# Windowed attention into a GELU MLP: from the fourth tile of tokens on, the first MLP product as seven block products instead of eight, with queries and keys loaded by pairs of heads

## The chip, the cores and the metric

The kernel runs on one core of one Trainium2 chip. The time is the device time of one execution in microseconds (us), median of three runs. The core has the engines PE (TensorE matmuls; PEld is its weight loads), DVE (VectorE), ACT (ScalarE), POOL (GpSimd), and SP, whose queue issues the DMAs.

## The reference

```python
# q, k, v: (8, 8, 576, 64) f32; w_in: (512, 2048), w_out: (2048, 512) f32
scores = scale * np.matmul(q, k.transpose(0, 1, 3, 2))
rel = pos[:, None] - pos[None, :]
scores = np.where((rel >= 0) & (rel < 128), scores + slopes * -abs(rel), -1e9)
attn = softmax(scores);  o = np.matmul(attn, v)
x = o.transpose(0, 2, 1, 3).reshape(8 * 576, 512)        # 4608 tokens
h = x @ w_in
return (0.5 * h * (1.0 + erf(h / sqrt(2)))) @ w_out      # (4608, 512)
```

## The kernel before

The 4608 tokens are cut into nine tiles of 512 (`t` = 0 to 8; the fourth tile is `t` = 3). The attention of batch 0 and the second product of tile 0 run in float32; elsewhere every float32 factor is kept as a float16 high part and a float16 low part, and a product is three matmuls (high by high, low by high, high by low) that add up in PSUM.

A tile has two phases. The h phase, `mlp_in(t, fc)` for 16 blocks `fc` of 128 hidden columns, adds 12 matmuls of 512 moving columns (4 blocks of the contraction by 3 terms) in one PSUM bank with the tag "mm" (four banks). ACT then applies GELU out of PSUM into a float32 buffer `g32` (tag "ob", three buffers), POOL writes its scaled float16 high part into `g`, and DVE writes the low part (`low_part`). The o phase, `mlp_out(t, tb, fc)`, computes four blocks of 128 tokens, each of 16 by 3 matmuls of 512 columns with `g` as the stationary operand, and stores them through a buffer of the same tag "ob".

Between these matmuls the attention of batch `b = t + 1` is placed by step: `scores(unit(b, hp))` of a pair of heads `hp` (54 small matmuls; DVE takes them out of PSUM with scale and bias into `s`), `softmax` (DVE maxima `nmax`, ACT exponentials, POOL high parts and DVE low parts in `e_main`, and two DMA transposes into `et`), and `weigh` (matmuls of `et` and `vbuf` into the bank `av`, then ACT and DVE write the high and low parts of `x` of this tile and the next one). `load_qk(b + 1)` fetches all queries and all keys of a batch at once into two large buffers (tag "ld"); `split_qk` measures them on DVE, sets a scale by a power of two, and writes the high and low parts into `qbuf` and `kbuf`. `split_v` does the same with the values.

The steps of one tile and the step at which each unit starts are a table (`SCORES_AT`, `WEIGH_AT`), but the order of instructions on each engine is set by a list scheduler that runs at build time: it may move an instruction ahead of others by its estimate of when the operands are there. Each engine then runs its list strictly in order, and SP issues the DMAs in order too.

## Time and profile before

| what | us |
|---|---|
| median of three runs | 959.24 (958.87 to 961.88) |
| the profiled execution | 957.65 |
| its span on the core | 955.8 |
| PE busy | 920.2 (96%) |
| DVE busy | 634.8 (66%) |
| ACT busy | 449.5 (47%) |
| POOL busy | 253.5 (27%) |

The profile is one execution. A line of a group gives the source line, the engine, the operation, what it writes and reads, the shapes, the count, then the busy time and the mean duration (ns) of one, then the idle time of the engine just before such instructions and what ended it. In the table by stretch each engine has its busy time in us and the number of its instructions; PEclk is the granted share of the TensorE clock. The phases stand cleanly apart in the trace: the tiles start at 187.9 (`t` = 1), 294.1, 395.8, 493.7, 592.2, 689.2, 786.1 and 869.0 us, and the last matmul starts at 951.7 us. A matmul's end is modelled, so time per matmul is read from start to start.

### The profile page before, as it was taken

The numbers are of one execution on the slowest core, as the hardware profiler recorded it, in microseconds if no ns is written. First come the engines' busy times: TensorE is split into PE (matmuls) and PEld (weight loads), VectorE is DVE, ScalarE is ACT, GpSimd is POOL, SyncE is SP. The second block draws the span as 40 slices with busy tenths as digits, with TensorE's granted clock in tenths as the row PEclk, the third lists the DMA queues.
The fourth block names the chain that finished last, engine by engine and source line by source line (L and its number), as shares of the span: only waits on it lengthen the run. The fifth ranks groups of instructions, "written<-read, shape, count | busy, mean of one in ns | idle before, by whom it ended". The sixth has DMA issues, their size and how long they took to land.

```text
span 955.8 us, 17566 instructions
## 1 busy us (share of the span) xinstructions
PE 920.2 (96%) x7036; PEld 450.0 (47%) x7036; DVE 634.8 (66%) x1254; ACT 449.5 (47%) x957; POOL 253.5 (27%) x516
## 2 busy tenths in 40 slices
PE   6979999899798999999999999999999999999998
PEld 3554444444454445444544445444544454444443
DVE  6899989769886978588767876777566722201200
ACT  5977556344563665256626643664366313101200
POOL 1010004323441533144313530353044312201200
PEclk8999999899999999999999999999999999999999
DMA  9527615762367424713371346245312430000000
GB/s 324 199 96 244 222 50 74 132 188 100 72 135 166 76 51 106 193 32 66 79 193 45 66 95 171 56 79 95 73 28 51 86 81 1 1 23 23 0 12 34
DMA packets 172451, 91.18 MB, mean 95 GB/s; under 512 B 132561, under 2 KB 153169, under 8 KB 172241
## 3 DMA queue, kind: packets, MB, share of 16 engines
q1 hardware_dynamic: 172368, 90.06, 38.3%
q8 instruction: 55, 0.90, 0.4%
q14 instruction: 28, 0.22, 0.1%
HBM read 46.53 MB, written 9.44 MB: 59 GB/s over the span
## 4 chain that ended last, share of the span: by engine, by line
PE 68%; DVE 8%; ACT 4%; DMA 3%; issue 2%; POOL 1%; SPq 0%; POOLq 0%; ACTq 0%; DVEq 0%
PE o L622 31%; PE h L584 29%; PE av L540 4%; PE sc L399 3%; DMA et<-e_main 2%; ACT s L494 2%; DVE e_main L145 2%; DVE s L421 1%; DVE g L145 1%; DVE nmax L491 1%; DVE stq L213 1%; POOL e_main L500 1%; DMA q<-qp 1%; DVE wo L145 1%; DMA v<-vp 1%
## 5 line engine op out<-in xcount | busy, mean ns | idle before, releaser
L584 PE MATMUL h<-x,wi 128*128 128x512 f16 x1728 | 381.8, 379 | 5.0 <-ACT g L600 3.3
L584 PEld LDWEIGHTS <-wi 128*128 128x128 f16 x1728 | 166.2, 98 | 205.8 <-issue 7.3
L622 PE MATMUL o<-wo,g 128*128 128x512 f16 x1152 | 260.2, 380 | 0.0
L622 PEld LDWEIGHTS <-g 128*128 128x128 f16 x1536 | 145.9, 98 | 175.2 <-issue 0.7
L601 POOL TENSOR_SCALAR g<-g,sg 128x512 f16<-128x512 f32 x128 | 104.2, 818 | 286.1 <-ACT g L600 280.4
L494 ACT ACTIVATE s<-s,nmax 128x192 f32<-128x192 f32 x252 | 111.2, 442 | 121.4 <-DVE nmax L491 114.4
L145 DVE SCALAR_TENSOR_TENSOR g<-g,sg,g 128x512 f16<-128x512 f32 x128 | 106.1, 841 | 90.4 <-POOL g L601 90.3
L500 POOL TENSOR_SCALAR e_main<-s,z 128x192 f16<-128x192 f32 x252 | 121.4, 499 | 126.1 <-issue 43.6
L600 ACT ACTIVATE g<-h,gs 128x512 f32<-128x512 f32 x128 | 86.0, 686 | 135.0 <-PE h L584 108.6
L145 DVE SCALAR_TENSOR_TENSOR e_main<-s,z,e_main 128x192 f16<-128x192 f32 x252 | 111.0, 482 | 15.3 <-POOL e_main L500 14.8
L622 PE MATMUL o<-wo_first,g 128*128 128x512 f16 x384 | 88.3, 379 | 0.0
L399 PE MATMUL sc<-kbuf,qbuf 64*64 64x192 f16 (+1 forms) x1656 | 73.3, 261 | 8.5 <-DMA kbuf<-kp 4.6
L421 DVE SCALAR_TENSOR_TENSOR s<-sc,cs,bias_h 128x384 f32<-128x384 f32 x112 | 63.6, 607 | 12.2 <-PE sc L399 12.0
L553 ACT ACTIVATE x<-av,cx 128x448 f16<-128x448 f32 (+6 forms) x52 | 23.8, 475 | 91.7 <-PE av L540 91.5
L491 DVE TENSOR_REDUCE nmax<-s 128x5 f32<-128x960 f32 (+1 forms) x56 | 58.5, 1044 | 2.7 <-DVE s L421 0.5
L619 PE MATMUL o<-zo,g 128*128 128x512 f32 x128 | 58.1, 606 | 0.0
L540 PE MATMUL av<-et,vbuf 128*64 128x128 f16 (+1 forms) x1680 | 46.0, 215 | 11.9 <-DMA et<-e_main 11.1
L426 POOL MEMSET s<- 64x128 f32 (+1 forms) x112 | 19.1, 171 | 135.1 <-DVE s L421 134.5
L630 ACT ACTIVATE ob<-o,so 128x512 f32<-128x512 f32 x16 | 10.8, 677 | 90.8 <-PE o L622 90.7
L399 PEld LDWEIGHTS <-qbuf 64*64 64x64 f16 x1512 | 36.2, 107 | 36.8 <-issue 33.5
L540 PEld LDWEIGHTS <-vbuf 128*64 128x64 f16 x1680 | 43.0, 114 | 22.2 <-issue 18.4
L632 DVE TENSOR_SCALAR ob<-o,so 128x512 f32<-128x512 f32 x16 | 11.9, 744 | 60.0 <-PE o L622 60.0
(129 smaller groups left out, 737.5 us busy)
## 6 DMA issues: line engine op xcount, KB each, us to landing
v<-vp SPq DMA_DIRECT2D x32, 320.0 KB, 5.2
out<-ob SPq DMA_DIRECT2D x36, 256.0 KB, 2.0
raw<-w_in SPq DMA_DIRECT2D x8, 1024.0 KB, 14.2
raw<-w_out SPq DMA_DIRECT2D x8, 1024.0 KB, 5.0
q<-qp SPq DMA_DIRECT2D x7, 1152.0 KB, 6.1
k<-kp SPq DMA_DIRECT2D x7, 1152.0 KB, 6.0
qbuf<-qp SPq DMA_DIRECT2D x4, 288.0 KB, 4.7
kbuf<-kp SPq DMA_DIRECT2D x4, 288.0 KB, 5.0
```

The source lines that it names most:

```text
L145: nc.vector.scalar_tensor_tensor(out=dst, in0=src, scalar=scale, in1=high, op0=ALU.mult, op1=ALU.subtract)
L399: nc.tensor.matmul(ps[bank][o, n, 0:W], a, m, start=(i == 0), stop=(i == len(terms) - 1 and b > 0), skip_group_check=True,)
L421: nc.vector.scalar_tensor_tensor(out=s[:, bank[0] : bank[0] + k, :], in0=ps[bank][:, 0:k, 0:W], scalar=cs, in1=bias.broadcast_to([P, k, W] ...
L491: nc.vector.tensor_reduce(out=nmax[:, r], in_=s[:, r], axis=AX.X, op=ALU.max, negate=True)
L494: nc.scalar.activation(s[:, i, :], s[:, i, :], AF.Exp, bias=nmax[:, i : i + 1], accum_out=z[:, i : i + 1])
L500: nc.gpsimd.tensor_scalar(e[:, i, 0, c], s[:, i], z[:, i : i + 1], 1.0, op0=ALU.mult, op1=ALU.mult)
L540: nc.tensor.matmul(av[r, (j - blocks[0]) * QB : (j - blocks[0] + len(js)) * QB], v32s[b][:, hp, kb, r] if b < EXACT else vbuf[:, vi, hp, k ...
L584: nc.tensor.matmul(ph, wi[n][:, a, cc, k * P : (k + 1) * P], x[:, cc, b, :], start=(i == 0), stop=(i == 3 * NCC - 1),)
L600: nc.scalar.activation(g32, ph, AF.Gelu, scale=gsc[t, n])
L601: nc.gpsimd.tensor_scalar(g[:, r, 0], g32, gsg[t, n], 1.0, op0=ALU.mult, op1=ALU.mult)
L619: nc.tensor.matmul(o, g[:, r, c], zo[n][:, n % 2, k * DM : (k + 1) * DM], start=(fc == 0), stop=(fc == NFC - 1))
L622: nc.tensor.matmul(o, g[:, r, a, c], wo[n][:, b, k, :], start=(fc == 0 and i == 0), stop=(fc == NFC - 1 and i == 2),)
```

## The change

Both halves of a block of the first product's operands are used in a scheme of seven products for a 2 by 2 by 2 product of blocks. Two token halves (`HT` = 256), two halves of the contraction (the blocks `2i` and `2i + 1` for `i` = 0, 1), and two blocks of 256 hidden columns (`wi[2d]` and `wi[2d + 1]`) make eight block products; for `t` >= `FAST` = 3 a class `Seven(t, d)`, `d` = 0 to 3, computes them with seven, `p1` to `p7`, each of 12 matmuls with 256 moving columns. They need sums of blocks:

- of the weights, formed once while tile 2 is computed (`sums_of_weights(d, i)`, eight calls, at the steps `SUMS_AT`). One sum replaces half of `wi[2d + 1]`; three go to DRAM (`stored`) and come back, for each `d` of each tile, by `stream` into `ldbuf`.
- of `x`, formed for each tile by `sums_of_x(t + 1, i)` during the tile before (POOL five additions, ACT high part, DVE low part).

The products of one `d` share two PSUM banks, `u` and `v`. A result is copied out, and the next product is added to what stands in the bank: `u` holds p1, then p1+p6, then also p7, then also p4; `v` holds p2, then (overwritten) p5, then also p3. ACT copies `u` out three times per `d`, DVE adds `v` to a copy three times, and four GELUs of [128, 512] with POOL and DVE parts follow as before.

Queries and keys of the batches from `WHOLE` = 3 on are held two pairs at a time (in half of `qbuf` and `kbuf`), because `ldbuf` is needed for the sums. From batch 4 on each pair is loaded twice: once into `src32[1]` to be measured, once into `src32[0]` to be split. One DVE chain `scales(b)` finds the scales of values, queries and keys together. The two weight blocks of a pair share a scale. `maxima` is taken out of `softmax`, and in the fast tiles the softmax of units whose scores fall in the h phase is held back until the o phase (`waiting`). The table `AT` moves the first unit of the next batch into the end of the tile before: tile 2 has five units of scores, tile 6 has three.

```diff
+WHOLE = 3
+FAST = 3
+HT = TT // 2
...
+    def load_pair(b, hp, n):
+        nc.sync.dma_start(src32[n][:, 0], qp[b, hp])
+        nc.sync.dma_start(src32[n][:, 1], kp_[b, hp])
+    def measure(b, hp):
...
+        absmax(stats[b][:, :, hp], src32[1])
...
+    def split_pair(b, hp):
...
+            nc.scalar.activation(a[:, 0:S], src, AF.Copy, scale=sc[:, n : n + 1])
+            low_part(a[:, S : 2 * S], src, sc[:, n : n + 1], a[:, 0:S])
...
+    def sums_of_weights(d, i):
+        r = ldbuf[:, LD : LD + 1024].rearrange("p (m c f) -> p m c f", m=2, c=2)
...
+        for m in range(2):
+            w = wi[2 * d + m]
+            nc.gpsimd.tensor_tensor(
+                out=r[:, m], in0=w[:, 0, 2 * i : 2 * i + 2], in1=w[:, 1, 2 * i : 2 * i + 2], op=ALU.add
+            )
+        b11, b21, b12, b22 = r[:, 0, 0], r[:, 0, 1], r[:, 1, 0], r[:, 1, 1]
+        nc.gpsimd.tensor_tensor(out=b11, in0=b12, in1=b11, op=ALU.subtract)
...
+        nc.scalar.copy(hi, flat)
+        nc.vector.tensor_tensor(out=lo, in0=flat, in1=hi, op=ALU.subtract)
+        nc.sync.dma_start(wi[2 * d + 1][:, :, 2 * i], st[:, :, 0])
+        for n, k in ((T2, 3), (T3, 2), (T4, 1)):
+            nc.sync.dma_start(stored[n, d, :, :, i], st[:, :, k])
+    def stream(n, d):
+        nc.sync.dma_start(streams[n], stored[n, d])
+    def sums_of_x(t, i):
+        x = x_tile(t)[:, 2 * i : 2 * i + 2]
+        r = pool.tile([P, 2, TT], F32, tag="s", name=f"r{t}_{i}", bufs=2)
+        nc.gpsimd.tensor_tensor(out=r, in0=x[:, :, 0], in1=x[:, :, 1], op=ALU.add)
...
+        nc.scalar.copy(hi, flat)
+        nc.vector.tensor_tensor(out=lo, in0=flat, in1=hi, op=ALU.subtract)
+    class Seven:
...
+        def add(self, ps, w, m, first):
+            n = 0
+            for k in range(2):
+                for i in range(2):
+                    for a, b in ((0, 0), (1, 0), (0, 1)):
+                        nc.tensor.matmul(
+                            ps[:, k * HT : (k + 1) * HT], w(a, i)[:, k * P : (k + 1) * P], m(b, i),
+                            start=first and n == 0, stop=True, skip_group_check=True,
+                        )
+                        n += 1
...
+        def p6(self):
+            self.add(self.u, lambda a, i: streams[T2][:, a, i], lambda b, i: sums[:, i, b, S2], False)
+            self.s2 = held2[self.d % 2]
+            nc.scalar.copy(self.s2, self.u)
...
+        def p7(self):
+            self.add(self.u, lambda a, i: streams[T3][:, a, i], lambda b, i: sums[:, i, b, S3], False)
+            s3 = self.room("s3")
+            nc.scalar.copy(s3, self.u)
+            nc.vector.tensor_tensor(out=s3, in0=self.v, in1=s3, op=ALU.add)
+            self.out(1, 1, s3)
...
+    AT = ((8, 14, 18, 22), (17, 22, 26, 30)), ((2, 11, 16, 21), (12, 20, 25, 30)), ((4, 8, 15), (14, 19, 22, 25))
+    NEXT_AT = 25
+    SUMS_AT = (4, 6, 8, 10, 12, 14, 16, 18)
```

The scheduler's order shows the change at two places. The first is tile 8, the start of the h phase, on PE. Before, one bank `h8_0` is filled by 12 matmuls of 512 columns (`x8` moving, `wi0` stationary), and the next matmuls go to another bank, `h8_1`:

```order
L584 LDWEIGHTS wi0_675
L584 MATMUL h8_0_9948<-x8_8710,wi0_675 128x512
L584 LDWEIGHTS wi0_675
L584 MATMUL h8_1_9966<-x8_8710,wi0_675 128x512
L584 LDWEIGHTS wi0_675
```

After the change, at the end of p7 and the start of p4 of `d` = 0 (`u8_0` is the bank, `ldbuf` holds the streamed sums and the sums of `x`):

```order
L784 LDWEIGHTS ldbuf_77
L784 MATMUL u8_0_11001<-ldbuf_77 128x256
L784 LDWEIGHTS ldbuf_77
L784 MATMUL u8_0_11001<-x8_9810,ldbuf_77 128x256
L784 LDWEIGHTS ldbuf_77
```

The twelve matmuls of p4 follow p7's twelve into the same bank, with nothing between them in this tile; in the tiles with attention, score matmuls stand there.

On ACT at that place stood a GELU for each bank before:

```order
L600 ACTIVATE g32_8_0_9962<-h8_0_9948,gs8_0_9942 128x512
L600 ACTIVATE g32_8_1_9979<-h8_1_9966,gs8_0_9942 128x512
L600 ACTIVATE g32_8_2_9996<-h8_2_9983,gs8_0_9942 128x512
L600 ACTIVATE g32_8_3_10013<-h8_3_10000,gs8_0_9942 128x512
L600 ACTIVATE g32_8_4_10031<-h8_4_10017,gs8_0_9942 128x512
```

and now (`s18_0` to `s48_0` are the buffers of p1, p7 and p4's results, `ldbuf` that of p6's):

```order
L805 COPY s18_0_11014<-u8_0_11001 128x512
L795 ACTIVATE s18_0_11014<-s18_0_11014,gs8_0_10991 128x512
L816 COPY ldbuf_77<-u8_0_11001 128x512
L824 COPY s38_0_11071<-u8_0_11001 128x512
L805 COPY s18_1_11091<-u8_1_11078 128x512
L795 ACTIVATE s38_0_11071<-s38_0_11071,gs8_0_10991 128x512
L795 ACTIVATE s18_1_11091<-s18_1_11091,gs8_0_10991 128x512
L795 ACTIVATE s48_0_11122<-u8_0_11001,gs8_0_10991 128x512
```

Three copies per `d` joined the four GELUs, and each copy stands between two products that use its bank.

The second place is tile 2, its h phase, on POOL. Before, between the high parts of hidden block 4 and of block 8 (`g2_1`, `g2_2` of `g32_2_4` to `g32_2_8`), stood the exponentials' high parts (`e_main`) and a fill of the mask (`s3_0`):

```order
L601 TENSOR_SCALAR g2_1_3375<-g32_2_4_3376,sg2_0_3239 128x512
L426 MEMSET s3_0_3306 64x64 x2
L601 TENSOR_SCALAR g2_1_3375<-g32_2_5_3461,sg2_0_3239 128x512
L500 TENSOR_SCALAR e_main_83<-s3_0_3306,z3_0_3411 128x192 x5
L601 TENSOR_SCALAR g2_1_3375<-g32_2_6_3478,sg2_0_3239 128x512
L500 TENSOR_SCALAR e_main_83<-s3_0_3306,z3_0_3411 128x192 x4
L601 TENSOR_SCALAR g2_1_3375<-g32_2_7_3527,sg2_0_3239 128x512
L601 TENSOR_SCALAR g2_2_3544<-g32_2_8_3545,sg2_0_3239 128x512
```

and now, from block 4 to block 7 (`ldbuf` is where the sums of the weights `wi2`, `wi3` are formed):

```order
L678 TENSOR_SCALAR g2_1_3351<-g32_2_4_3352,sg2_0_3213 128x512
L730 TENSOR_TENSOR ldbuf_77<-wi2_707 128x512
L730 TENSOR_TENSOR ldbuf_77<-wi3_710 128x512
L734 TENSOR_TENSOR ldbuf_77<-ldbuf_77 128x256
L498 MEMSET s3_0_3278 64x64 x2
L735 TENSOR_TENSOR ldbuf_77<-ldbuf_77 128x256
L736 TENSOR_TENSOR ldbuf_77<-ldbuf_77 128x256
L678 TENSOR_SCALAR g2_1_3351<-g32_2_5_3452,sg2_0_3213 128x512
L737 TENSOR_TENSOR ldbuf_77<-ldbuf_77 128x256
L678 TENSOR_SCALAR g2_1_3351<-g32_2_6_3475,sg2_0_3213 128x512
L578 TENSOR_SCALAR e_main_86<-s3_0_3278,z3_0_3401 128x192 x5
L678 TENSOR_SCALAR g2_1_3351<-g32_2_7_3507,sg2_0_3213 128x512
```

The additions of a set of weight sums stand among the high parts of `g`, five of them between blocks 4 and 5.

More of the change, by code (lines that the diff above doesn't have):

```diff
@@ L706, in attention_gelu_mlp @@
     split_tail()
[L707 to L710 removed]
+    for hp in range(2):
+        all_scores(unit(1, hp))
+        maxima(unit(1, hp))
+        softmax(unit(1, hp))
     scores_at, weigh_at, split_at = {1: 2, 3: 3}, {2: 0, 4: 1, 6: 2}, {5: 0, 6: 2, 7: 4}
@@ L746, in attention_gelu_mlp @@
                 continue
             if step in at:
-                hp, i = at[step]
-                scores(unit(b, hp), BANKS[PIECES[i]])
+                u, i = at[step]
+                st = unit(*divmod(u, NPAIR))
+                scores(st, BANKS[PIECES[i]])
                 if i == 2:
-                    softmax(unit(b, hp))
+                    maxima(st)
+                    if fast and step <= len(first):
+                        waiting.append(st)
+                    else:
+                        softmax(st)
@@ L752, in attention_gelu_mlp @@
+            if step == len(first) + 1:
+                for st in waiting:
+                    softmax(st, held2[1][:, 0:NG])
             if step == 1:
```

262 lines of the change are left out of this document (214 added, 48 removed).

## The prediction

> **What bounds the kernel now.** The page first, its busy shares and slices, to see whether one engine leads all through:
>
> ```profile
> PE 920.2 (96%) x7036; PEld 450.0 (47%) x7036; DVE 634.8 (66%) x1254; ACT 449.5 (47%) x957; POOL 253.5 (27%) x516
> ...
> PE   6979999899798999999999999999999999999998
> ...
> DVE  6899989769886978588767876777566722201200
> ```
>
> PE leads; DVE is next, and only until tile 7. Then the table by stretch, cut at the tiles named in the front (1, second half of 1, 2, 3, 4, 5, 6, 7), to see what PE lacks in each:
>
> ```profile
> 187.90:294.10 106.20, 99.12 (x829) 49.23 (x828) 86.42 (x174) 47.59 (x107) 37.09 (x69) 0.98 0.52 132
> 236.50:294.10 57.60, 52.69 (x493) 27.12 (x493) 49.81 (x109) 27.18 (x84) 21.59 (x51) 0.97 0.57 118
> 294.10:395.80 101.70, 99.10 (x920) 48.40 (x918) 77.08 (x153) 52.34 (x113) 34.06 (x68) 1.00 0.48 106
> 395.80:493.70 97.90, 97.57 (x817) 47.12 (x816) 74.84 (x150) 50.97 (x112) 32.75 (x68) 1.00 0.43 98
> 493.70:592.20 98.50, 97.07 (x865) 46.95 (x864) 73.94 (x150) 51.44 (x112) 32.56 (x68) 1.00 0.42 97
> 592.20:689.20 97.00, 97.00 (x818) 46.84 (x816) 70.17 (x150) 53.12 (x113) 33.05 (x68) 1.00 0.38 75
> 689.20:786.10 96.90, 96.90 (x841) 46.89 (x840) 57.86 (x111) 45.50 (x109) 32.48 (x68) 1.00 0.30 61
> 786.10:869.00 82.90, 82.90 (x385) 37.56 (x384) 13.74 (x19) 13.65 (x19) 11.15 (x16) 1.00 0.04 13
> ```
>
> After the length come PE, PEld, DVE, ACT, POOL, the granted clock, the DMA share. From tile 3 on PE idles 0.3, 1.4 and then 0 us: a matmul less is a shorter tile, as long as the others keep up. In tile 2 it idles 2.6 us; in the second half of tile 1, with DVE at 49.81 / 57.60 = 86%, it idles 4.9 us. The waits of PE from 187 us on say for whom:
>
> ```profile
> PE av L540 <- DMA et<-e_main: 6.7, 2, 4.1
> PE h L584 <- ACT g L600: 3.3, 2, 1.8
> ```
>
> So PE waits at the end of the softmax chain or for GELU to empty a bank, never for weights.
>
> **The change, part by part.**
>
> *Matmuls.* Per tile 192 of 512 columns become 4 x 7 x 12 = 336 of 256. Prices from the timeline (start, length, count), start to start:
>
> ```profile
> 786.13 14.19 PE L584 MATMUL h<-x,wi 128*128 128x512 f16 x65
> ...
> 33.08 0.81 PE L474 MATMUL tp<-bias_h,adders 128*128 128x384 bf16 x4
> ...
> 33.41 0.49 PE L474 MATMUL tp<-bias_h,adders 128*128 128x384 bf16 x2
> ...
> 505.25 2.27 PEld L584 LDWEIGHTS <-wi 128*128 128x128 f16 x12
> ...
> L584 PE MATMUL h<-x,wi 128*128 128x512 f16 x1728 | 381.8, 379 | 5.0 <-ACT g L600 3.3 <-ACT g L597 1.2 <-ACT x L553 0.3
> L584 PEld LDWEIGHTS <-wi 128*128 128x128 f16 x1728 | 166.2, 98 | 205.8 <-issue 7.3
> ```
>
> 512 columns: (14.19 - 0.379) / 64 = 0.216 us. 384 columns: (0.81 - 0.49) / 2 = 0.16. The line through both gives 0.11 at 256 columns (0.108 in proportion); no row has 256. Every matmul has its own load of 98 ns, which starts with the matmul before: 98 < 110, so it stays hidden, by a margin of a tenth. If load and matmul stood one after the other, 384 columns would take 0.26, which the rows exclude. I take 0.1095: 336 x 0.1095 = 36.8 against 192 x 0.216 = 41.4, so 4.6 us less per tile, 27.8 us in six tiles. Ends: 0.108 (5.1 per tile) and 0.115 (2.8).
>
> *Reading the shared bank.* ACT's copy of 512 columns is priced by GELU from PSUM, DVE's addition by the output's scaling from PSUM:
>
> ```profile
> L600 ACT ACTIVATE g<-h,gs 128x512 f32<-128x512 f32 x128 | 86.0, 686 | 135.0 <-PE h L584 108.6 <-DVE g L145 17.1 <-DVE sx L140 4.3
> L632 DVE TENSOR_SCALAR ob<-o,so 128x512 f32<-128x512 f32 x16 | 11.9, 744 | 60.0 <-PE o L622 60.0
> L601 POOL TENSOR_SCALAR g<-g,sg 128x512 f16<-128x512 f32 x128 | 104.2, 818 | 286.1 <-ACT g L600 280.4 <-DVE turned L118 3.3 <-DVE s L421 2.1
> L500 POOL TENSOR_SCALAR e_main<-s,z 128x192 f16<-128x192 f32 x252 | 121.4, 499 | 126.1 <-issue 43.6 <-ACT s L494 32.4 <-ACT x L553 27.1
> L145 DVE SCALAR_TENSOR_TENSOR wi<-zi,sww,wi 128x1024 f16<-128x1024 f32 x8 | 10.2, 1288 | 0.0
> ```
>
> Between most products on one bank the order puts 18 to 36 others (2 to 4 us), which hide a 0.69 us copy. At tile 8, `d` = 0, p4 follows p7 directly: the matmul's tail (0.379 - 0.216 = 0.16) plus 0.69 plus a hand-over, about 1.0 us of PE idle; tile 7 has the same order: 1.0 us each. In tiles 3 to 6 score matmuls stand in that gap (32 x 53.9 / 1512 = 1.1 us, rows below); tile 6 still gets 1.0 us, as tile 4 now idles 1.4.
>
> *VectorE.* Per fast tile: 12 additions x 0.744 = 8.9 us, and two low parts of the sums of `x`, 2 x 1.288 = 2.6; the pairwise measuring and splitting moves as many elements as before. So 11.5 us more in tiles 3 to 6. Tile 2 gains eight low parts of weight sums (10.3 us), 2.6 for `x`, and the fifth unit, priced by these rows (four scalings 0.607 and one 0.409, maxima 2.09, nine low parts 0.482: 9.3, with its small ones 9.7):
>
> ```profile
> L421 DVE SCALAR_TENSOR_TENSOR s<-sc,cs,bias_h 128x384 f32<-128x384 f32 x112 | 63.6, 607 | 12.2 <-PE sc L399 12.0
> L421 DVE SCALAR_TENSOR_TENSOR s<-sc,cs,bias_p 128x192 f32<-128x192 f32 x28 | 11.5, 409 | 10.6 <-PE sc L399 10.5
> L491 DVE TENSOR_REDUCE nmax<-s 128x5 f32<-128x960 f32 x28 | 32.2, 1150 | 2.4 <-DVE s L421 0.5
> L491 DVE TENSOR_REDUCE nmax<-s 128x4 f32<-128x768 f32 x28 | 26.3, 938 | 0.3 <-POOL s L426 0.2
> L145 DVE SCALAR_TENSOR_TENSOR e_main<-s,z,e_main 128x192 f16<-128x192 f32 x252 | 111.0, 482 | 15.3 <-POOL e_main L500 14.8
> L399 PE MATMUL sc<-kbuf,qbuf 64*64 64x192 f16 x1512 | 53.9, 249 | 1.3 <-DVE s L421 1.3
> ```
>
> DVE work then: tile 2 77.1 + 22.6 = 99.7; tile 3 74.8 + 11.5 = 86.3; tile 4 85.4; tile 5 81.7; tile 6 57.9 + 11.5 - 9.7 = 59.7. Without PE waits tile 2 would last 101.7 - 2.6 + 1.9 (a unit's scores: 53.9 / 28) = 101.0, tile 3 97.6 - 4.6 = 93.0, tile 4 92.5, tile 5 92.4: DVE shares of 99%, 93%, 92%, 88%. Here the saving is spent again. What is late when DVE is late: the addition that frees `v` for p5, or the one ahead of p3, and at the tile's end the low part of `g`. The nearest row for such a load is the 86% stretch, with 4.9 of 57.6 us lost. I take waits of 6 us in tile 2, 3 in tile 3, 2 each in tiles 4 and 5. Ends: no waits, and a DVE that never passes 86%.
>
> *GpSimd.* The weight sums are 16 additions of 512 and 32 of 256. The one-input rows give 0.818, and 0.563 on the line through 512 and 192: 31.1 us in tile 2; sums of `x` 7.2, the unit 4.5. POOL then works 34.1 + 42.8 = 76.9 of 107 us, hidden unless bunched. The "GPSIMD Engine Reference" of the Trainium skill (section 3.1) has a two-input addition bound by a single read port, at 4497 ns for 2048 elements. By that the 20,480 elements of both kinds of sums would cost an estimated 45 us instead of 38.3, and POOL would still fit; no row here has a two-input operation on POOL. Ends: as the row, and twice the row (rival 3).
>
> *DMA.* A stream of 256 KB is nearest to this issue row (KB, us to landing):
>
> ```profile
> qbuf<-qp SPq DMA_DIRECT2D x4, 288.0 KB, 4.7
> ```
>
> Between p6 of one `d` and of the next lie seven products, 9.2 us, which hide 4.7. SP issues streams, pair loads and transposes in one order; a pair load waits for DVE's low part of the pair before it, and the streams behind it wait too. About 4 us are left for that. 0, with DVE's lateness already charged. ACT gains 12 x 0.69 + 2 x 1.3 = 11 us on 51 of 98: hidden.
>
> *Shared scales, maxima apart, first tiles.* The same or fewer instructions; 0, within 2 us either way by the order of tile 1.
>
> *Sum* against the profiled execution (957.65; the median of the runs is 1.6 above it, and I add the difference to the median): tile 2 101.0 + 6 - 101.7 = +5.3; tile 3 93.0 + 3 - 97.9 = -1.9; tile 4 92.5 + 2 - 98.5 = -4.0; tile 5 -2.6; tile 6 -4.6 - 1.9 + 1.0 = -5.5; tiles 7 and 8 -3.6 each. Together -15.9: 959.2 - 15.9 = 943.3.
>
> **The rivals.**
>
> 1. *No waits remain.* All 27.8, and the 4.3 us that PE idles in tiles 2 to 4 also go: 927. For it: the held-back softmax takes DVE work out of the h phase. Against: DVE at 88 to 99%, which PE outran at 86%.
>
> 2. *VectorE sets the length of tiles 2 to 5.* Their DVE work is 353.1 us, their length before 395.1; the other tiles give 12.7. At 86% they last 410.6, together 962; at the 81% of tile 1 (86.42 / 106.20) 433.8, together 985. Break-even is 353.1 / 407.8 = 86.6%; my forecast needs 90%. At 84% it is 972, slower than before. For it: g's low part waits for POOL and ACT and DVE is in order. Against: much of DVE's work in the o phase can be late. The skill's "Advanced Engine Details and Errata" says that the second Vector SBUF port is shared with GpSimd and that the two can block each other; the addition from PSUM cannot show it, no run here separates it, and it would only push the same way.
>
> 3. *Two-input additions on POOL cost twice the row.* Tile 2 then has 34.1 + 4.5 + 76.6 = 115 us of POOL work, 8 us more than my 107: 951. For it: five additions stand between the high parts of two hidden blocks. Against: three buffers and four banks let PE run ahead by several blocks of 2.6 us.
>
> 4. *The matmuls do not shrink.* At 0.123 us each 336 cost 41.4 again, and the kernel ends at 971. Against: the 384-column row.
>
> **How the numbers follow.** My forecast, 935 to 950, 0.42; rival 1 (925 to 935) 0.18; rival 3 (948 to 955) 0.16; rival 2 0.22, of which 0.08 stays within 0.3% (2.9 us, about what a measurement can tell from no change), 0.02 just below and 0.12 above; rival 4 0.02. Faster 0.78, same 0.08, slower 0.14. The range 926 to 961 leaves out the upper half of rival 2 and the lowest edge of rival 1.
>
> **What would show it.** Start to start of the 256-column matmuls at 0.109 us, h phases of tiles 7 and 8 near 37.8 us; DVE at about 93% of tile 2 and 90% of tiles 3 to 5; tile 2 longer than before; additions on POOL near 0.8 us for 512. Wrong if PE waits over 4 us per tile for DVE in tiles 3 to 5, if matmuls take over 0.115 us, or if streams land late.

## Result and the profile after

| | before | after |
|---|---|---|
| median, us | 959.06 (957.18 to 961.88) | 1014.66 (1011.84 to 1019.29) |
| profiled execution, us | 957.65 | 1015.99 |
| its span, us | 955.8 | 1014.2 |

The ratio is 1.058, with a 95% interval of 1.053 to 1.063: the kernel became slower by 55.6 us, where 16 us less was forecast. By the starts of the tiles in the two traces:

| stretch | before | after | difference | forecast |
|---|---|---|---|---|
| start to tile 2 | 294.1 | 310.0 | +15.9 | 0 |
| tiles 2 and 3 | 199.6 | 237.5 | +37.9 | +3.4 |
| tiles 4 to 6 | 292.4 | 304.9 | +12.5 | -12.1 |
| tiles 7 and 8 | 165.6 | 157.7 | -7.9 | -7.2 |

Only the last row came as forecast. Everything before it lost time. The page of the changed kernel, with the lines that answer to those of before:

```profile
PE 921.9 (91%) x7900; PEld 543.6 (54%) x7900; DVE 727.3 (72%) x1314; ACT 475.0 (47%) x1049; POOL 378.0 (37%) x633
...
PE   7967998999897878799997999899979999999998
...
DVE  6898988669884999869887868786876672620520
```

PE is busy for as long as before (920.2), though the products shrank, and it idles 92 us instead of 36. The table by stretch, cut at tiles 1 to 8 (columns as before: length, PE, PEld, DVE, ACT, POOL, granted clock, DMA share):

```profile
203.00:310.00 107.00, 100.95 (x818) 48.34 (x817) 86.26 (x159) 51.04 (x113) 44.76 (x81) 0.97 0.54 137
310.00:447.10 137.10, 109.74 (x919) 52.09 (x918) 114.91 (x182) 66.39 (x147) 87.49 (x123) 0.90 0.61 154
447.10:547.50 100.40, 95.76 (x962) 62.46 (x961) 83.57 (x155) 50.50 (x124) 43.84 (x78) 1.00 0.56 140
547.50:651.70 104.20, 97.21 (x1010) 63.14 (x1009) 82.11 (x155) 50.39 (x123) 46.20 (x81) 0.97 0.56 125
651.70:753.50 101.80, 95.72 (x962) 62.73 (x961) 79.42 (x155) 50.37 (x123) 43.78 (x81) 0.98 0.50 119
753.50:852.40 98.90, 93.01 (x932) 61.37 (x931) 62.77 (x111) 40.51 (x98) 47.87 (x79) 0.98 0.42 92
852.40:931.30 78.90, 78.23 (x529) 51.60 (x528) 26.68 (x34) 23.18 (x34) 18.57 (x23) 1.00 0.19 54
931.30:1010.10 78.80, 78.08 (x529) 51.54 (x527) 22.59 (x30) 19.16 (x30) 11.39 (x16) 1.00 0.15 44
```

Tile 2 is the worst, 137.1 us against 101.7: PE idles 27 us in it, and works 109.7 where 101.0 was forecast, at a granted clock of 0.90. DVE works 114.9 us, not 99.7. In tile 6, though, DVE is busy for only 63% and the tile still grew, so one full engine does not explain all of it. The waits of PE from tile 2 on:

```profile
PE sc L471 <- DVE s L493: 19.0, 11, 5.7
PE av L618 <- DMA et<-e_main: 9.5, 4, 7.2
PE u L784 <- ACT s L805: 7.5, 2, 4.5
PE sc L471 <- DVE x L149: 7.0, 4, 2.7
PE v L784 <- ACT ob L707: 4.9, 1, 4.9
```

From tile 2 on PE idles 52.4 us. Half of that, 26.0 us, is scores that wait for DVE (to empty their banks, `s` L493, or for a low part of `x`), which no step of the prediction named. The transposes at the end of the softmax chain take 9.5 us, and the products `u` and `v` that wait for ACT take 12.4 us in the two largest lines.

### The profile page after: what moved, and what is told of

Same layout as the page of the kernel before. It is cut to its first block, busy times and chain, and to the rows that moved or that the text cites. A ratio compares the mean times of both kernels' runs of the same rounds, so it can differ in the third digit from the quotient of the medians.

```text
span 1014.2 us, 19995 instructions
## 1 busy us (share of the span) xinstructions
PE 921.9 (91%) x7900; PEld 543.6 (54%) x7900; DVE 727.3 (72%) x1314; ACT 475.0 (47%) x1049; POOL 378.0 (37%) x633
## 3 DMA queue, kind: packets, MB, share of 16 engines
q8 instruction: 62, 1.02, 0.4%
## 4 chain that ended last, share of the span: by engine, by line
PE 37%; DVE 23%; ACT 8%; POOL 8%; DMA 6%; issue 5%; SPq 1%; DVEq 0%; POOLq 0%; ACTq 0%
PE o L699 14%; PE u L784 10%; PE v L784 7%; DVE e_main L149 7%; ACT s L572 4%; DMA et<-e_main 4%; POOL e_main L578 4%; PE h L661 3%; DVE nmax L559 3%; DVE s L493 2%; DVE g L149 2%; DMA kbuf<-kp 2%; PE sc L471 2%; POOL r L753 1%; DMA v<-vp 1%
## 5 line engine op out<-in xcount | busy, mean ns | idle before, releaser
L699 PE MATMUL o<-wo,g 128*128 128x512 f16 x1152 | 267.7, 387 | 0.0
L578 POOL TENSOR_SCALAR e_main<-s,z 128x192 f16<-128x192 f32 x252 | 133.4, 547 | 90.4 <-ACT s L572 29.4
L572 ACT ACTIVATE s<-s,nmax 128x192 f32<-128x192 f32 x252 | 111.1, 442 | 98.7 <-DVE nmax L559 85.7
L149 DVE SCALAR_TENSOR_TENSOR e_main<-s,z,e_main 128x192 f16<-128x192 f32 x252 | 134.6, 578 | 27.2 <-POOL e_main L578 27.2
L661 PE MATMUL h<-x,wi 128*128 128x512 f16 x576 | 131.4, 385 | 9.8 <-ACT g L674 4.1
L471 PE MATMUL sc<-kbuf,qbuf 64*64 64x192 f16 (+1 forms) x1656 | 81.8, 266 | 39.7 <-DVE s L493 24.6
L798 POOL TENSOR_SCALAR g<-s,sg 128x512 f16<-128x512 f32 x72 | 55.5, 776 | 126.3 <-ACT s L795 111.4
L784 PEld LDWEIGHTS <-ldbuf 128*128 128x128 f16 x864 | 84.2, 100 | 26.6 <-issue 10.8
L784 PE MATMUL u<-ldbuf 128*128 128x256 f16 x576 | 74.8, 280 | 8.4 <-ACT s L805 7.5
L149 DVE SCALAR_TENSOR_TENSOR g<-s,sg,g 128x512 f16<-128x512 f32 x72 | 59.7, 846 | 25.3 <-POOL g L798 25.2
L784 PE MATMUL v<-ldbuf,wi 128*128 128x256 f16 x576 | 70.1, 275 | 0.2 <-DVE s L810 0.2
L493 DVE SCALAR_TENSOR_TENSOR s<-sc,cs,bias_h 128x384 f32<-128x384 f32 x112 | 64.0, 605 | 1.7 <-PE sc L471 1.2
L618 PEld LDWEIGHTS <-vbuf 128*64 128x64 f16 x1680 | 43.9, 115 | 25.2 <-DMA et<-e_main 11.5
```

What stands on the lines that cost most here:

```text
L149: nc.vector.scalar_tensor_tensor(out=dst, in0=src, scalar=scale, in1=high, op0=ALU.mult, op1=ALU.subtract)
L471: nc.tensor.matmul(ps[bank][o, n, 0:W], a, m, start=(i == 0), stop=(i == len(terms) - 1 and b > 0), skip_group_check=True,)
L493: nc.vector.scalar_tensor_tensor(out=s[:, bank[0] : bank[0] + k, :], in0=ps[bank][:, 0:k, 0:W], scalar=cs, in1=bias.broadcast_to([P, k, W] ...
L572: nc.scalar.activation(s[:, i, :], s[:, i, :], AF.Exp, bias=nmax[:, i : i + 1], accum_out=z[:, i : i + 1])
L578: nc.gpsimd.tensor_scalar(e[:, i, 0, c], s[:, i], z[:, i : i + 1], 1.0, op0=ALU.mult, op1=ALU.mult)
L618: nc.tensor.matmul(av[r, (j - blocks[0]) * QB : (j - blocks[0] + len(js)) * QB], v32s[b][:, hp, kb, r] if b < EXACT else vbuf[:, vi, hp, k ...
```

## The experiments

The starts of the tiles in each trace give the lengths of the four stretches. All are in us. "time" is a median of 4 to 12 executions for before, after, e4, e9, e10 and e13 and one execution for the others; the medians of the kernel before beside them were 957.5 to 961.3, and its 23 executions beside e9 to e11 lay between 954.8 and 964.8. So a few us in one row can be chance, in a stretch too: up to 85 us, e9 and the kernel before have the same order of instructions on DVE, and the same step (the inverse of the last scales) starts at 87.9 us in one trace and at 85.4 in the other.

| run | time | start to tile 2 | tiles 2 and 3 | tiles 4 to 6 | tiles 7 and 8 |
|---|---|---|---|---|---|
| before | 959.06 | 294.1 | 199.6 | 292.4 | 165.6 |
| after | 1014.66 | 310.0 | 237.5 | 304.9 | 157.7 |
| e1_no_seven | 990.76 | 309.1 | 216.1 | 294.1 | 165.6 |
| e8_no_measure | 967.71 | 306.9 | 195.9 | 293.0 | 165.6 |
| e2_no_weight_adds | 1001.51 | 309.4 | 222.4 | 306.1 | 157.8 |
| e5_fills | 1003.54 | 304.8 | 230.0 | 305.1 | 157.8 |
| e3_no_x_adds | 989.17 | 307.6 | 230.5 | 287.0 | 157.8 |
| e14_x_on_vector | 1016.16 | 310.2 | 240.4 | 301.7 | 157.7 |
| e6_shared_scale | 976.26 | 310.9 | 201.5 | 292.3 | 165.6 |
| e7_ring | 966.87 | 300.9 | 202.7 | 291.7 | 165.6 |
| e10_spare_op | 958.14 | 293.9 | 199.6 | 291.6 | 165.6 |
| e13_scale_merged | 961.91 | 301.5 | 197.1 | 291.6 | 165.6 |
| e11_three_out | 965.76 | 306.2 | 208.8 | 287.2 | 157.7 |
| e4_late7 | 990.78 | 315.7 | 200.1 | 307.0 | 162.1 |
| e9_late8 | 957.19 | 301.5 | 197.5 | 292.0 | 161.6 |

### Without the seven products: e1_no_seven

```diff
-FAST = 3
+FAST = 99
...
-                if t + 1 < NTILE and step in (len(first) + 1, len(first) + 4):
+                if FAST <= t + 1 < NTILE and step in (len(first) + 1, len(first) + 4):
```

By the same constant the fifth unit of tile 2 and the softmax that is held back are gone as well: each tile has four units, as before. What stays of the change is the loading by pairs, the shared scale, the buffer in turns and the maxima taken out of `softmax`.

> The changed kernel with eight products in every tile: no class Seven, no sums of weights or of x, no streams; queries and keys by pairs, shared weight scales and the moved softmax stay. If the sums and products alone cost the time of tiles 2 to 6, tile 2 falls from 137 to about 104 us and tiles 3 to 6 to about 97 each, while the first 310 us (16 later than before at the start of tile 2) stay as they are: about 975 us. If loading and splitting by pairs is what hurts, tiles 2 to 5 stay over 105 us: 995 or more.

Measured: 990.76, 29.5 us above the kernel before although no product is changed. 15.0 of them lie ahead of tile 2, 16.5 in tiles 2 and 3. That lies between the two times expected: tiles 2 and 3 stayed long (111.1 and 105.0 us), tiles 4 to 6 did not. So half of the loss belongs to what was costed at nothing: the loading by pairs, the shared scale and the first tiles.

### The measuring by pairs: e8_no_measure

This is e1_no_seven without the first load of each pair and without its maxima; a constant stands for what they found.

```diff
-                    if step:
-                        measure(b + 1, step // 2 - 1)
-                    if step < 8:
-                        load_pair(b + 1, step // 2, 1)
+                    if b + 1 not in stats:
+                        stats[b + 1] = small([P, 2, NPAIR], f"sta{b + 1}", 1, tag="sta")
+                        nc.vector.memset(stats[b + 1], 4.0)
```

> The run with eight products in every tile (pairs, shared scale and moved softmax kept), without the first load of each pair and without its measuring: the largest values of queries and keys of batches 4 to 7 are set to a constant. If loading and measuring by pairs made tiles 2 and 3 9 and 7 us longer there, they fall from 111 and 105 to about 102 and 98: about 974 us. If it is the splitting by pairs and the earlier first unit, they stay over 107 and 102.

Measured against e1: tiles 2 and 3 took 195.9 us instead of 216.1, 20.2 less, and 3.7 less than before; 98.0 and 97.9 us are the two tiles, where 102 and 98 were expected. The splitting by pairs, which stayed, costs nothing that shows; the measuring by pairs costs it all, 16.5 us of it beyond what the measuring of before cost (199.6 has that in it, 195.9 has none). DVE's waits for these loads in tiles 2 and 3 of e1_no_seven:

```profile
DVE sta L227 <- DMA kbuf<-kp: 15.8, 8, 3.7
```

In the changed kernel, DVE's group of these maxima in tile 2, with the idle time behind the second bar:

```profile
L227 DVE TENSOR_REDUCE sta<-kbuf 128x2 f32<-128x1152 f32 x9 | 12.2, 1351 | 11.5 <-DMA kbuf<-kp 11.5
```

The program places four of these in each of tiles 2 to 5. The scheduler moved them ahead, nine into tile 2. There they share one staging buffer: each waits for its load, the next load waits for it, and DVE, which runs in order, stands still 11.5 us while PE waits for it to empty score banks. e8 takes out the loads, DVE's waits for them and the maxima themselves (1.35 us each) together; what each is worth alone was not measured. Before, maxima over whole loads made the same measurement; in tile 2 these were three, with 7.2 us of waits. Two of them:

```profile
L213 DVE TENSOR_REDUCE stq<-k 128x1 f32<-128x2304 f32 x2 | 5.1, 2553 | 5.0 <-DMA k<-kp 5.0
```

### GpSimd's sums of the weights: e2_no_weight_adds, e5_fills

The first leaves the additions out, the second puts fills that keep GpSimd busy about as long in their place (48.9 us in all; the additions took 46.6):

```diff
-            nc.gpsimd.tensor_tensor(
-                out=r[:, m], in0=w[:, 0, 2 * i : 2 * i + 2], in1=w[:, 1, 2 * i : 2 * i + 2], op=ALU.add
-            )
...
-        nc.gpsimd.tensor_tensor(out=b11, in0=b12, in1=b11, op=ALU.subtract)
...
+            nc.gpsimd.memset(fr[:, 0:700], 1.0)
+            nc.gpsimd.memset(fr[:, 0:700], 1.0)
...
+            nc.gpsimd.memset(fr[:, 0:900], 1.0)
```

> The changed kernel without the six GpSimd additions in each set of weight sums (the copy, the low part and the stores stay; the sums are then wrong). If GpSimd's two-input additions slow VectorE's operations that read two SBUF tensors, e_main's low part in tile 2 falls from 644 to about 500 ns and tile 2 from 137 to about 108 us: about 986 us in all. If tile 2 is long for VectorE's own added work (fifth unit, measuring, splitting, low parts), it stays at 125 us or more.

> The changed kernel with each GpSimd addition of the weight sums replaced by fills of about the same time (two of 700 elements for each addition of 512, one of 900 for each of 256; the sums are then wrong). GpSimd is as busy in tile 2, but reads nothing. If tile 2 is long because these additions block VectorE's second read port, it falls from 137 to near the 120 us without additions, and e_main's low part in it to about 550 ns. If it is GpSimd's time and order, tile 2 stays over 132 us.

Measured in tiles 2 and 3: 237.5 us with the additions, 230.0 with fills, 222.4 with neither. The additions cost 15.1 us over the two tiles. The two tiles tell different things. Tile 2, in which most of the sums are formed, took 137.1 us with additions, 121.9 with fills and 119.9 with neither (about 108 had been expected for e2, near 120 for e5): there GpSimd's time costs 2.0 us, and what the additions do beside keeping it busy costs 15.2. Tile 3, in which no fill stands, took 100.4, 108.1 and 102.5; the largest wait of e5 there is 4.6 us of PE for ACT's cast of the sums of `x`. The table by stretch of tile 2, of e5 and of e2 (114.91 us of DVE in the changed kernel):

```profile
304.80:426.70 121.90, 104.39 (x919) 50.64 (x918) 100.32 (x176) 62.99 (x144) 87.33 (x135) 0.94 0.61 156
309.40:429.30 119.90, 102.97 (x923) 49.28 (x920) 99.18 (x182) 64.83 (x145) 49.33 (x87) 0.97 0.66 175
```

With fills GpSimd is as busy as with additions (87.3 and 87.5 us), but DVE works 14.6 us less; with neither it works 15.7 less. The groups by shape in tile 2 tell where. The low part of the exponentials on DVE, which has two inputs in SBUF, in before, after, e5 (fills) and e2 (neither):

```profile
L145 DVE SCALAR_TENSOR_TENSOR e_main<-s,z,e_main 128x192 f16<-128x192 f32 x37 | 15.4, 456 | 1.7 <-POOL e_main L500 1.6
```
```profile
L149 DVE SCALAR_TENSOR_TENSOR e_main<-s,z,e_main 128x192 f16<-128x192 f32 x45 | 26.9, 644 | 3.1 <-POOL e_main L578 3.1
L493 DVE SCALAR_TENSOR_TENSOR s<-sc,cs,bias_h 128x384 f32<-128x384 f32 x20 | 11.3, 604 | 0.1
L730 POOL TENSOR_TENSOR ldbuf<-wi 128x512 f32<-128x512 f16 x12 | 15.2, 1290 | 6.1 <-DVE ldbuf L741 6.1
L734 POOL TENSOR_TENSOR ldbuf<-ldbuf 128x256 f32<-128x256 f32 x6 | 6.1, 1023 | 0.3
```
```profile
L149 DVE SCALAR_TENSOR_TENSOR e_main<-s,z,e_main 128x192 f16<-128x192 f32 x41 | 20.6, 542 | 1.3 <-POOL e_main L578 1.3
```
```profile
L149 DVE SCALAR_TENSOR_TENSOR e_main<-s,z,e_main 128x192 f16<-128x192 f32 x45 | 21.0, 505 | 2.5 <-POOL e_main L578 2.5
```

With the additions a low part takes 644 ns; with fills 542, with neither 505. (The 456 of before is no measure for the additions: in e11 below, which has none at all, it is 507.) The low part of `g` goes the same way: 909, 783 and 784 ns. The scaling of the scores (L493), of the same operation but with one input in PSUM, takes 604, 606 and 607 in the three, and 607 before. So DVE is slowed where it reads two operands from SBUF while GpSimd reads too. The Trainium skill says this in "SBUF — State Buffer" (section "Who interferes with whom"): a VectorE instruction with two SBUF inputs contends with a GpSimd instruction that reads SBUF, not with one that only writes. The trace agrees in the main: 644 beside readers and 542 beside fills, though the fills still stand 37 ns above the 505 with neither.

### GpSimd's sums of x: e3_no_x_adds, e14_x_on_vector

The first leaves the ten additions of `sums_of_x` out (high and low parts are taken of `x` itself), the second moves them to VectorE. Of the second, the first of five lines:

```diff
 # e14
-        nc.gpsimd.tensor_tensor(out=r, in0=x[:, :, 0], in1=x[:, :, 1], op=ALU.add)
+        nc.vector.tensor_tensor(out=r, in0=x[:, :, 0], in1=x[:, :, 1], op=ALU.add)
```

> The changed kernel without the GpSimd additions in the sums of x (the high and low parts are taken from x itself, so the sums are wrong). If the long chain of additions at the end of a tile makes PE wait at p6 of the next tile, the waits of 4.6, 3.2 and 5.1 us at the start of tiles 4, 5 and 6 vanish and tiles 4 to 6 are 3 to 5 us shorter each: about 1002 us. If VectorE's share sets the length of these tiles, they lose less than 2 us each: 1010 us.

> The changed kernel with the ten additions per tile of the sums of x on VectorE instead of GpSimd (about 5.5 us of VectorE per tile). Theory (in tiles 4 to 6 the loss of 18 us comes from GpSimd's slow additions, behind which ACT's cast of the sums, and behind that the copies that empty the bank u, stand in order): tiles 4 to 6 together 290 to 297 us against 304.9, though VectorE works 5 us more in each. Rival (VectorE's load is what counts there): tiles 4 to 6 stay at 303 us or get longer.

Measured: without them tiles 4 to 6 took 287.0 us, 17.9 less than after and 5.4 less than before, and the three waits at their starts are gone. Tiles 2 and 3 became 7.0 us shorter as well, so the time is 989.2 where 1002 was expected. What they do at the start of tile 4 the timelines of ACT, of POOL and of PE in the changed kernel show (start, length; the idle time before it in brackets):

```profile
554.89 1.04 ACT L761 CAST ldbuf<-r 128x1024 f16<-128x1024 f32 x1 [6.54 <-POOL r L758]
555.84 0.58 ACT L805 COPY s<-u 128x512 f32<-128x512 f32 x1
```
```profile
545.18 2.13 POOL L753 TENSOR_TENSOR r<-x 128x1024 f32<-128x1024 f16 x1 [1.41 <-DVE z L576]
547.29 4.39 POOL L578 TENSOR_SCALAR e_main<-s,z 128x192 f16<-128x192 f32 x4
551.64 0.81 POOL L755 TENSOR_TENSOR r<-r 128x256 f32<-128x256 f32 x1
```
```profile
551.40 0.60 PE L784 MATMUL v<-x,wi 128*128 128x256 f16 x4
556.47 0.81 PE L784 MATMUL u<-ldbuf 128*128 128x256 f16 x5 [4.47 <-ACT s L805]
```

GpSimd's five additions run from 545 to past 553 with four high parts between them. ACT has the cast of their result next in its list and waits 6.5 us; the copy that empties `u` stands behind that cast, and p6 waits for the copy. Tiles 5 and 6 begin in the same way: casts that wait 5.1 and 8.2 us, and PE behind them 3.0 us for the copy of `u` and 4.9 for ACT's copy of an output block (`ob`), which stands behind the cast in tile 6.

On VectorE the same additions gave 301.7, between the two expectations. Tile 6 got what was expected (92.4 against 98.9 us; DVE has room there). Tiles 4 and 5 did not (104.3 and 105.0 us, against 104.2 and 101.8 after): DVE works 82.7 and 82.4 us there, 79 and 78% of the tile, and now scores wait for it, 8.8 us in tiles 4 to 6 where it was 4.6. Neither engine takes the sums for free there.

### The start: e6_shared_scale, e7_ring, e10_spare_op, e13_scale_merged

All four are the kernel before with one edit (constants that go with it are left out below): the scale shared by a pair of weight blocks; the buffer `ldbuf` taken in turns in place of the pool's "ld"; an operation like that of the first that nothing reads; the shared scale again, with its maximum merged into an operation that is there.

```diff
 # e6
+        nc.vector.tensor_tensor(out=stat[:, 0:1], in0=stat[:, 0:1], in1=stat[:, 1:2], op=ALU.max)
-        pow2_of_words(pww[:, r], stat)
+        pow2_of_words(pww[:, r], stat[:, 0:1].broadcast_to([P, len(ns)]))
...
 # e7
...
-                zz = pool.tile([P, 2, NW], F32, tag=tag, name=f"zi{n}", bufs=bufs)
+                    zz = ld(2 * NW).rearrange("p (n f) -> p n f", n=2)
...
 # e10
+        nc.vector.tensor_tensor(out=spare, in0=stat[:, 0:1], in1=stat[:, 1:2], op=ALU.max)
 # e13 (in place of the floor and of e6's maximum)
+        nc.vector.tensor_scalar(stat[:, 0:1], stat[:, 0:1], stat[:, 1:2], STAT_FLOOR, op0=ALU.max, op1=ALU.max)
```

> The kernel before with one scale for two weight blocks (one more small VectorE operation per pair) and nothing else changed. If the late start of the changed kernel (16 us at tile 2) comes from the shared scale, tile 1 starts at 195 us or later instead of 188; if from the buffer with turns, it starts at 188 to 190 and the time is 960 us.

> The kernel before with its pool of two large buffers replaced by one buffer whose halves are taken in turns, and nothing else changed. If the late start comes from that buffer (transfers and scales wait for the whole of it, or stand later in the order), tile 1 starts at 195 us or later; if from the shared scale, at 188 to 190 and the time is 960 us.

> The kernel before, with one more operation for each pair of weight blocks at the start: the maximum of two [128, 1] columns on VectorE (four operations in all, each about 0.1 us), written to a buffer that nothing reads. Theory (what the shared scale costs at the start comes from the order that the list scheduler then chooses, not from sharing a scale): tile 2 starts several us later than the 294.2 of before, up to the 310.9 that the shared scale gave. Rival (a shared scale makes the first weights wait for both blocks of the pair): tile 2 starts at 294 to 296 and the kernel takes 959 to 961 us.

> The kernel before with the shared scale of the weight pairs, but the maximum of the two blocks is taken in the operation that applies the floor, so that VectorE's chain from the measured maximum to the scale has as many dependent steps as before (floor, exponent, inverse). Theory (what costs the start is the added dependent step: on a busy, in-order VectorE each such step is put behind one or two operations of 1.2 us, and the splitting of the second pair of weights came 7 to 10 us later with it): the splitting of the second pair at 60 to 64 us, tile 2 starts at 293 to 299 us, the kernel takes 957 to 964. Rival (sharing a scale between two blocks costs it by itself, because both must be measured first): tile 2 starts at 308 to 311 us, the kernel takes 974 to 977.

Measured: the shared scale alone brings the whole delay (tile 1 at 206.9, tile 2 at 310.9). The ring, the buffer taken in turns, costs 9 us alone, 6.8 of them ahead of tile 2, but tile 1 starts at 184.2 there, 3.7 us earlier than before, so neither branch of what was expected holds; the 6.8 us do not add to the delay, since the changed kernel with both is at 310.0. An operation that nothing waits for costs nothing (293.9): that went against what was expected. Merged into the floor, the shared scale costs 3.5 us (ratio 1.0032, interval 1.0004 to 1.0060) instead of 18.7. Tile 2 starts at 301.5 there, where 293 to 299 was expected: of the 16.8 us that e6 starts it late, 9.4 go with the added step and 7.4 are left. The timeline of DVE in e6 shows the chain of the second pair (floor, maximum, exponent, inverse, then the two low parts of the weights):

```profile
53.37 0.16 DVE L111 TENSOR_SCALAR stw<-stw 128x2 f32<-128x2 f32 x1
...
55.85 0.15 DVE L235 TENSOR_TENSOR stw<-stw 128x1 f32<-128x1 f32 x1
...
58.32 0.16 DVE L208 TENSOR_SCALAR pww<-stw 128x2 int32<-128x2 int32 x1
...
62.73 0.15 DVE L140 TENSOR_SCALAR sww<-pww 128x2 int32<-128x2 int32 x1
...
69.28 2.47 DVE L145 SCALAR_TENSOR_TENSOR wi<-zi,sww,wi 128x1024 f16<-128x1024 f32 x2
```

and in e13, where the maximum is in the floor:

```profile
51.33 0.20 DVE L234 TENSOR_SCALAR stw<-stw 128x1 f32<-128x1 f32 x1
53.87 0.16 DVE L208 TENSOR_SCALAR pww<-stw 128x2 int32<-128x2 int32 x1
56.34 0.16 DVE L140 TENSOR_SCALAR sww<-pww 128x2 int32<-128x2 int32 x1
...
62.00 2.47 DVE L145 SCALAR_TENSOR_TENSOR wi<-zi,sww,wi 128x1024 f16<-128x1024 f32 x2
```

Each step takes 0.16 us of DVE, but DVE is full here (28.0 of the 28 us from 48 to 76 in e6), and the list scheduler puts other work, mostly 1.2 us apiece, between two steps that depend on each other. One dependent step more is 2.5 us or more for each pair, and all that shares DVE's list comes later. PE's longest waits from 60 to 110 us in e6, in which before had 1.4 us in all:

```profile
PE tp L476 <- DVE x L145: 4.4, 1, 4.4
PE h L586 <- ACT g L599: 3.7, 1, 3.7
```

They are named after `x` and a GELU, not after the weights: it is the list as a whole that fell behind. The 7.4 us that are left in e13 are not the lateness of these weights: in e10 the two low parts of the second pair start at 62.20 us, as late as in e13, and tile 2 is not late. e9 below starts tile 2 at 301.5 as well, with the scales of before. So a delay of this size comes with another order of the list too, and what makes it, and what in the ring costs 9 us, stays open.

### Do the causes add up: e11_three_out

It joins the edits of e2_no_weight_adds, e3_no_x_adds and e8_no_measure in the changed kernel.

> The changed kernel with three of its additions left out together: GpSimd's additions in the sums of the weights, those in the sums of x, and the first load and measuring of queries and keys by pairs (a constant stands for what was measured). The seven products, their copies and VectorE additions, the streams, the split by pairs and the shared scale stay. Theory (the causes add up): tile 2 starts near 308 as in the changed kernel; tiles 2 and 3 together 202 us (237.5 - 15.1 - 20.2), tiles 4 to 6 287 us, tiles 7 and 8 157.8; the span about 961 us, the time about 963. Rival (the causes are not separate: VectorE stays in order behind the seven products' own additions): tiles 2 to 6 together 500 us or more, against 489, and the time above 972.

Measured: 965.76, against the 963 expected. Tiles 4 to 6 and 7 to 8 came to the microsecond; tiles 2 and 3 took 208.8 instead of 202.2. That expectation left out the 7.0 us by which e3 had shortened tiles 2 and 3. The three savings measured singly there are 15.1, 20.2 (in the kernel without the seven products) and 7.0 us, together 42.3; taken out at once they gave 28.7. So in tiles 2 and 3 the causes overlap. In tiles 4 to 6 the 287 us are what e3 alone had given. The table by stretch of this run, tiles 2 to 6:

```profile
306.20:418.50 112.30, 102.28 (x919) 49.32 (x918) 89.28 (x172) 65.48 (x146) 42.31 (x81) 0.97 0.56 136
418.50:515.00 96.50, 94.00 (x962) 61.55 (x961) 78.85 (x156) 50.83 (x125) 32.91 (x70) 1.00 0.57 133
515.00:612.60 97.60, 94.25 (x1010) 61.62 (x1009) 75.71 (x156) 50.13 (x123) 33.05 (x70) 1.00 0.57 131
612.60:710.60 98.00, 95.43 (x962) 62.26 (x961) 76.18 (x156) 50.57 (x123) 32.82 (x70) 0.98 0.55 133
710.60:802.20 91.60, 91.35 (x932) 60.62 (x931) 55.02 (x107) 40.75 (x98) 27.71 (x57) 1.00 0.40 89
```

Tiles 3 to 6 idle 2.5, 3.3, 2.6 and 0.3 us. Yet even here, with free sums and free measuring, the change is worth little: tiles 2 and 3 +9.2, tiles 4 to 6 -5.2, tiles 7 and 8 -7.9, together 3.9 us gained, and the late start takes 12.1.

### Where the seven products pay: e4_late7, e9_late8

e4 is the changed kernel with the seven products in tiles 7 and 8 alone and whole loads of queries and keys (`WHOLE = B`, `FAST = 7`); its weight sums stand in tile 6, and the scales of tile 0 are formed at the place where before formed them. e9 is the kernel before with them in tile 8 alone. There the weights keep their own scales, and in tile 7, which has no attention, ACT brings them to a shared scale and the sums are formed:

```diff
+    def rescale(n):
+        w = wi[n].rearrange("p a c f -> p (a c f)")
+        nc.scalar.activation(w, w, AF.Copy, scale=late["f"][:, n : n + 1])
...
+            if t == FAST - 1 and step in SUMS_AT:
+                d, i = divmod(SUMS_AT.index(step), 2)
+                if i == 0:
+                    rescale(2 * d)
+                    rescale(2 * d + 1)
+                sums_of_weights(d, i)
```

> Seven products in tiles 7 and 8 alone; weight sums formed in tile 6; queries and keys loaded whole and split as in the kernel before; the scales of tile 0 formed where they were before; the shared scale of two weight blocks and the buffer with turns stay. Tiles 7 and 8 give 3.9 us each, as in the changed kernel. If the late start of the changed kernel comes from where the scales of tile 0 are formed, the start is as before and the time 950 to 956 us; if it comes from the shared scale or the buffer, the start stays up to 16 us late: about 966 us. Tile 6, with VectorE at 60%, may lose up to 8 us to the sums.

> The kernel before, with the seven products in tile 8 alone. The weights keep their own scales at the start; in tile 7, which has no attention, ACT brings the two weight blocks of a pair to a common scale by a power of two, and the sums of the weights and of x are formed there. Theory (the seven products themselves are worth what was forecast, 3.9 us in a tile without attention, and the loss lies in what prepares them on engines that are needed): tile 8 78.8 us against 82.7, tiles 0 to 7 as before within 1 us, since VectorE and ACT are idle for four fifths of tile 7; the kernel 955 us, 0.4% faster. Rival A (the scheduler's order at the start shifts with any edit): tile 2 starts 4 to 17 us later than before and the kernel ends at 959 to 972. Rival B (POOL's additions delay the high parts of g, or the sums land late): tile 7 or the start of tile 8 longer by 3 us or more, the kernel at or above 958.

Measured: e4 took 1.029 times the time of before (1.023 to 1.034). 966 was expected with a late start. It kept the late start (315.7), so the place of the scales of tile 0 is not its cause, and tile 6 with the sums took 110.5 us instead of 96.9 (up to 8 more had been expected), with DVE's low part at 642 ns there too. Tile 7, right behind the sums, gained nothing: 83.3 us against 82.9, 2.4 of them spent waiting for the sums of `x`. Tile 8 gave its 3.9. e9 took 0.9974 times (0.9958 to 0.9990; 957.19 against 960.08 beside it). It is 0.26% faster than the kernel before, a small gain whose interval leaves 1 out; no other run here has that. Its last two tiles:

```profile
790.90:873.70 82.80, 82.80 (x385) 37.52 (x384) 30.99 (x28) 38.54 (x37) 64.10 (x69) 1.00 0.22 67
873.70:952.50 78.80, 78.13 (x529) 51.55 (x527) 23.82 (x31) 19.40 (x31) 11.39 (x16) 1.00 0.17 51
```

All the sums run in tile 7, with POOL at 64 of 82.8 us, and PE does not idle at all there. The price of the preparation depends on the tile: nothing here, 13.6 us in tile 6. But tile 2 started 7.4 us later than before, though the program is the same up to tile 6: two small maxima of the weight scales, which only the late sums use, have their inputs early, and the scheduler put them at 88 us; DVE's order differs from there. Part of the 7.4 us, 2.5, is already there ahead of that point. Only 2 us came back in tiles 2 and 3. In the two profiled executions this used up the gain (spans of 956.6 and 955.8); over 12 and 23 executions 2.9 us were left of tile 8's 4.

## Why the prediction was wrong

**Right: the matmuls.** The timeline of PE in tile 8 of the changed kernel (start, length, operation, count):

```profile
931.31 1.47 PE L784 MATMUL u<-x,wi 128*128 128x256 f16 x12
932.62 1.47 PE L784 MATMUL v<-x,wi 128*128 128x256 f16 x12
...
939.17 1.47 PE L784 MATMUL u<-ldbuf 128*128 128x256 f16 x12
941.36 0.82 PE L784 MATMUL u<-x,ldbuf 128*128 128x256 f16 x6 [0.72 <-ACT s L824]
```

(932.62 - 931.31) / 12 = 0.109 us, as forecast, so rival 4, that the matmuls do not shrink, is out. From p7 to p4 it is 2.19 us instead of 1.31: 0.9 us of idle, forecast 1.0. Tiles 7 and 8 became 3.9 us shorter each; forecast was 3.6.

**Wrong: "Shared scales, maxima apart, first tiles. ... 0, within 2 us."** It was 15.9. The instructions were counted, not the length of the chain. e6, e10 and e13 show that one dependent step on a full DVE was the larger part of it (9.4 of the 16.8 us in e6); the rest goes with the order of the list and stays open.

**Wrong: "the pairwise measuring and splitting moves as many elements as before".** True of elements, and the splitting by pairs cost nothing that shows. The measuring cost 20 us (e1, e8). What the traces show of it is that waits for whole loads became a row of waits on one buffer, in an engine that runs in order. The prediction said that a pair load waits for DVE; it did not ask whether DVE waits for the load.

**Wrong: the sums on GpSimd "hidden unless bunched".** The sums of the weights cost 15.1 us in tiles 2 and 3 (e2), those of `x` 7.0 there and 17.9 in tiles 4 to 6 (e3). Three things were off. The additions were mis-sized: 1.29 us for 512 against 0.82, 0.80 to 1.02 for 256 against 0.56; the weight sums alone took 46.6 us, above even the 45 that the prediction named as the larger estimate for all the sums. DVE's rows were taken from a trace without additions beside them: its low parts, counted at 482 ns, take 644 with them and 505 without (e2). And what waits for the sums was not followed: ACT's work was called hidden by its total, but its cast waits for the sums, and behind the cast stands the copy that frees `u`.

**Wrong: DVE's 99.7 us in tile 2.** It was 114.9: 45 low parts at 0.644 us instead of 0.482 (7 us), nine maxima by pairs (12.2 us) where three of 2.55 had been counted in (4.5 us more), and the splitting of five pairs (10.2 us) where one whole batch of 5.4 had been counted in (4.8 us more). The low parts of the sums took 1.5 us less than counted.

**About right: the waits in tiles 3 to 6,** where nothing else disturbs: 3, 2, 2 for DVE and 1 for ACT's copy were taken, 2.5, 3.3, 2.6 and 0.3 measured in e11. The place was right as well: the largest of these waits, 4.8 us in three, is `v` waiting for DVE's addition of p7. But that the sizes agree is in part luck: DVE is at 82, 78 and 78% of tiles 3 to 5 of e11, not at the 93, 92 and 88% from which they were taken, and e11 lacks the additions of `x`. In tile 2 it is 10, not 6.

**The rivals.** Rival 2 came nearest in its numbers: tiles 2 to 5 have 360.0 us of DVE work in 443.5 us, 81%, and for 81% it gave 985, still 30 us short. It had 0.22, of which 0.12 slower. As a mechanism it is half of it: in e3 DVE has 76 and 79% of tiles 4 and 5, against 79 and 78% after, and they are 6.1 and 4.5 us shorter. So there what stands ahead of the needed instruction in the order counted, and not the share of busy time. Rival 3 had the direction (1.6 times the row for 512, not twice) but sought the loss in POOL's own time. The sentence on the second Vector port, "it would only push the same way", gave a mechanism of its own no price.

## What to carry to other kernels

Before counting matmuls saved, write down for every new preparing operation which engine's list it stands in, what it waits for there, and what stands behind it: a measurement, a cast or a sum that waits for its input holds up all that follows on that engine. A dependent step costs its place in a full engine's list, not its duration. Work that prepares a saving was free here only where the engines idle (tile 7 in e9), so start with the tile behind such a place and see whether it pays at all.

## What the runs showed of the hardware

- A VectorE operation with two SBUF inputs took 1.28 times as long in tile 2 with GpSimd's additions as without (644 and 505 ns, the changed kernel and e2), and 542 with fills; one with an input in PSUM did not change (604 and 607).
- Two-input additions on GpSimd took 1234 ns for 512 columns of f16 and 722 to 849 for 256 of f32 in e9, in a tile in which VectorE had 31 of 83 us of work, and 1290 and 795 to 1023 in tile 2 of the changed kernel.
- Where PE waited more, the granted clock was lower, and its matmuls took longer. Tiles 2 and 3 of e1 and of e8 have 1681 matmuls each; PE idled 16.5 us in e1 and was busy for 199.6 at a granted clock of 0.96, and it idled 1.4 us in e8 and was busy for 194.5 at 1.00. So 5 of the 20 us between them lie in PE's busy time and not in its waits:

```profile
309.10:525.20 216.10, 199.63 (x1681) 96.74 (x1680) 152.81 (x296) 105.57 (x236) 67.60 (x136) 0.96 0.51 121
```
```profile
306.90:502.80 195.90, 194.53 (x1681) 93.89 (x1680) 139.68 (x283) 105.06 (x235) 70.34 (x136) 1.00 0.47 98
```
